# Two split stores, new list-scheduler priorities and two moved products in a fused scan and mixture-of-adapters kernel

## The chip, the cores and the metric

The kernel runs on one core of one Trainium2 chip. The metric is device time in microseconds (us) of one execution, smaller is better. The kernel before was timed in three runs, and one more execution was profiled.

## What is computed

Two stages follow one another. The first is a linear recurrence over time on a batch of 8 sequences of 6400 steps with 128 channels. The second takes each of the 51200 rows of its result as a token, picks the 2 best of 8 adapters for it, and adds the weighted low-rank (rank 16) products to the token.

```python
for t in range(S):                      # a, b: (8, 6400, 128)
    h = a[:, t] * h + b[:, t]
    out[:, t] = h
x = out.reshape(B * S, D)               # (51200, 128)
logits = x @ w_gate                     # 8 adapters
topk = two best of the 8 logits
w = softmax over these two
delta = sum over the two of w * ((x @ A[e]) @ B[e])
return x + delta
```

## The kernel before

**Tiling.** The 51200 rows are cut into 100 units of 512 rows (`UT`). Channels lie on the partitions while the recurrence runs, so that one VectorE scan instruction handles 512 steps of all 128 channels; a sequence has 12.5 units, so four units hold a boundary and take two scans.

**One unit's work**, by the names that the planner uses:

- `lda`, `ldb`: loads of a and b into rings of 8 slots (`RING`), two units (512 KB) per transfer except for a few at the start and the end, issued from SyncE's queue.
- `AB`: sixteen TensorE transposes that turn a and b into channel-major PSUM tiles (`pA`, `pB`).
- `aev`: ScalarE copies a from PSUM to `a_st`. `scan`: VectorE writes `xT` in fp16, a ring of 16 units (`XR`).
- `L`: four small matmuls give logits in `pTL`; `lev` copies the logits of a whole gating group to `Lg`.
- `gating`: per group of up to four units, m1, p1, p2, p3, m2, p4 to p7 on VectorE and GpSimd find the two best logits and the argument of a sigmoid (`sig`, ScalarE), which gives the weights `g`. In the groups with `quick` (the first three and the last two, `QUICK`) an eight-way maximum (`mx`) takes the place of m1 to m2, and the elementwise steps may go to either engine.
- `Z`: four matmuls with all the adapters' A at once. `mul`: the product with the weights, on VectorE out of PSUM, or, for the units in `POOL_MULS`, on GpSimd; GpSimd cannot read PSUM, so ScalarE first copies `Z` to `z_sb` (`zev`).
- `T`: four transposes of the weighted product; `tev`: ScalarE copies them to `zwT`.
- `R` and `D`: the tokens themselves and the adapters' B are accumulated in `pO`; `oev` copies the sum to a slot of `outt` (24 slots, `NOUT`). For the last ten units VectorE may take this copy too.
- `st`: stores of two units (512 KB), single units at the two ends, issued from SyncE's queue.

**The order.** Nothing is written out by hand. Every operation is put into a `_Plan` with its engine, a cost, what it depends on, and a key: its unit plus the offset of its kind in `KEY`, and, from unit `N_LATE` on, also that in `LATE`. `schedule` is a list scheduler. It takes the engine on which something can start soonest, looks at all that could start there within the engine's `SLACK` (ns) of that time, and emits the one with the smallest key:

```python
limit = soonest[e0] + self.slack.get(e0, 0.0)
t, op, e, pick = min((f for f in found if f[2] == e0 and f[0] <= limit), key=lambda f: (f[1].key, f[0]))
```

Each engine then runs its list in that fixed order and waits on semaphores where a dependency is on another engine. The costs only decide the order. TensorE's instructions are emitted through a helper (`_Parts`), so all its matmuls have line 90 and all its transposes line 94 in the profile.

**Groups.** `cut(HEAD, 4, TAILS)` makes the gating groups: the sizes in `HEAD` first, then fours for what is left, then the sizes in `TAILS`:

```python
rest = NU - u - sum(sizes_tail)
while rest > 0:
    n = min(size, rest)
```

**Stores.** The store that begins with unit `u0` waits for the copies of its units and, as long as `u0 + HOLD` (22) is smaller than `FREE`, also for the scan of unit `u0 + HOLD`, so that loads come first. The copy of unit `v` waits until the store of unit `v - 24`, which used the same slot, has landed.

Of the kernel before, what the change touches and what calls it, by code (L numbers as in the profile page):

```python
# [10 lines left out]


KEY = {
    "AB": -125.2, "aev": 74.6, "scan": 73.9, "L": -8.3, "lev": -133.3, "gate": 36.0, "sig": 65.6, "Z": 82.1,
    "mul": -166.5, "zev": 37.9, "T": -103.7, "tev": -4.9, "R": 173.0, "D": 58.8, "oev": 185.5,
}
SLACK = {
    "pe": 0.0, "dve": 20.0, "act": 0.0, "pool": 300.0, "sp": 200.0,
}
HEAD = (1, 1, 2, 1, 1, 3)  # L20
TAILS = (4, 3)
QUICK = (3, 2)
POOL_MULS = (2, 3, 5, 7, 10, 12, 14, 17, 22, 26, 30, 34, 38, 42, 46, 50, 54, 58, 62, 66, 70, 74, 78, 84, 89, 90)
HOLD = 22
FREE = 100
HEATS = 7
WIDE = 100
SOLO = (2, 4)
# [4 lines left out]
NOUT = 24  # L33
TAIL = 10
FILLS = 1
OUT4 = 86
LATE = {
    "L": -48.5, "zev": 113.4, "tev": -1.9, "aev": 21.0, "lev": -59.3, "sig": 6.0, "gate": 31.5, "AB": 19.8,
    "scan": -3.5, "mul": -20.9, "T": -31.3,
}  # L40
N_LATE = 80


class _Op:
# [55 lines left out]
class _Plan:  # L100
# [9 lines left out]
    def add(self, name, eng, kind, unit, cost, emit, deps=(), dma=None, bank=None, mode=None):  # L110

        engs = (eng,) if isinstance(eng, str) else eng
        cost = cost if isinstance(cost, dict) else {e: cost for e in engs}
        self.ops[name] = _Op(name, engs, kind, unit, cost, emit, list(deps), dma, bank, mode)

    def schedule(self, first, link, landing, switch):
# [3 lines left out]
        for op in ops.values():  # L120
            op.deps = [ops[d] for d in dict.fromkeys(op.deps) if d in ops]
            left[op.name] = len(op.deps)
            op.key = op.unit + self.offset.get(op.kind, 0.0)
            if op.unit >= N_LATE:
                op.key += LATE.get(op.kind, 0.0)
# [89 lines left out]
def bass_associative_scan_2x2__then__mixture_of_adapters_kernel(  # L215
# [8 lines left out]
    NB, S, D = a.shape  # L224
    E = moe_w_gate.shape[1]
    R = moe_A.shape[2]
# [8 lines left out]
    NZ, NO = 2, 2  # L235
    ON_POOL = lambda v: v in POOL_MULS

    def cut(sizes_head, size, sizes_tail):
        got, u = [], 0
        for n in sizes_head:  # L240
            got.append((u, n))
            u += n
# [3 lines that stand above are left out]
            got.append((u, n))  # L246
            u += n
            rest -= n
        for n in sizes_tail:
            got.append((u, n))  # L250
            u += n
        return got

    groups = cut(HEAD, 4, TAILS)
    GM = max(n for _, n in groups)
# [3 lines left out]
    with ExitStack() as stack:  # L259
# [20 lines left out]
        outt = sb(nc.sbuf_tensor("outt", [128, NOUT, UT], F32))  # L280
# [30 lines left out]
        def add_dma(name, eng, unit, starts, slot, time, deps=()):  # L311

            if slot not in dma_sem:
                dma_sem[slot] = [sb(nc.semaphore("q_" + "_".join(map(str, slot)))), 0]
            dma_sem[slot][1] += 16 * len(starts)
            sem, value = dma_sem[slot]

            def emit(h):
                for dst, src in starts:
                    last = h.dma_start(dst, src).then_inc(sem, 16)  # L320
                return last

            add(name, eng, "dma", unit, (450.0 * len(starts), 0.0), emit, deps, (sem, value, time))
# [54 lines left out]
        def fill(w):  # L378


            def emit(h):
                for _ in range(3):
                    last = h.matmul(pO[1][:, :], warm_t[:, 0:128], warm_t[:, :])
                return last

            add(f"fill{w}", "pe", "fix", 1000.0, (600.0, 800.0), emit, [f"AB{w}"])

        for w in range(FILLS):
            fill(w)
# [398 lines left out]
        def t_evac(v):  # L788
# [8 lines left out]
                bank=t_bank(v),  # L797
            )

        def o_bank(v):  # L800
            return pO[v % NO] if v < OUT4 else (pO + pB)[(v - OUT4) % 4]

        def o_free(v):
            if v < OUT4 + 2:
                return f"oev{v - NO}"
            return f"scan{NU - 2 + v % 2}" if v < OUT4 + 4 else f"oev{v - 4}"

        def delta(v):
            def emit(what):
                def run(h):  # L810
                    for q, w in [(q, w) for q in range(Q) for w in what]:
                        left, right = {"x": (x_rows(v, q), ident_h[:, :]), "d": (zw_rows(v, q), Bcat_h)}[w]
                        last = h.matmul(
                            o_bank(v)[:, q * 128 : (q + 1) * 128],
                            left,
                            right,
                            start=w == "x" and q == 0,
                            stop=w == "d",
                            skip_group_check=True,
                        )  # L820
                    return last

                return run

            deps = [f"scan{mates(v)[-1]}", o_free(v), "idh"]
            if v == 1:
                deps += [f"fill{w}" for w in range(5)]
            tevs = [f"tev{w}" for w in mates(v)]
            if FUSE[0] <= v < FUSE[1]:
                add(f"D{v}", "pe", "D", v, (WIDE8, WIDE8 + 200.0), emit("xd"), deps + tevs + ["cstB"], mode="full")  # L830
            else:
                add(f"R{v}", "pe", "R", v, (223.0, 423.0), emit("x"), deps, mode="full")
                add(f"D{v}", "pe", "D", v, (220.0, 420.0), emit("d"), [f"R{v}", "cstB"] + tevs, mode="full")

        def o_evac(v):
            def emit(h):
                copy = h.tensor_copy if plan.ops[f"oev{v}"].eng == "dve" else h.copy
                return copy(outt[:, v % NOUT, :], o_bank(v)[:, :])  # L838

            tail = v >= NU - TAIL  # L840
            add(
                f"oev{v}",
                ("act", "dve") if tail else "act",
                "oev",
                v,
                {"act": (477.0, 645.0), "dve": (600.0, 745.0)} if tail else (477.0, 645.0),
                emit,
                [f"D{v}", f"st{store_of.get(v - NOUT)}"],
            )

        stores, u = [], 0
# [3 lines left out]
        store_of = {v: j for j, (u0, n) in enumerate(stores) for v in range(u0, u0 + n)}  # L855

        def store(j):
            u0, n = stores[j]
            s0 = u0 % NOUT
            rows = out[u0 * UT : (u0 + n) * UT, :].rearrange("(p i) d -> p (i d)", p=128)  # L860
            add_dma(
                f"st{j}",
                "sp",
                u0 + HOLD,
                [(rows, outt[:, s0 : s0 + n, :].rearrange("p n c -> p (n c)"))],
                ("o", s0, n),
                1.036 * ((625.0 if n == 2 else 650.0) * n + 13.0),
                [f"oev{v}" for v in range(u0, u0 + n)] + [f"scan{u0 + HOLD}"] * (u0 + HOLD < FREE),
            )

        for w in range(NU):
            for t in "ab":
# [6 lines left out]
        for v in range(NU):  # L879
            logits(v)  # L880
            z_mm(v)
            z_mul(v)
            zw_tr(v)
            t_evac(v)
            delta(v)
            o_evac(v)
        for k in range(len(groups)):
            gating(k)
        for j in range(len(stores)):
            store(j)  # L890
        ends = [f"st{j}" for j in range(len(stores) - NOUT, len(stores))]
        add("end", "sp", "fix", 1.0e9, (10.0, 10.0), lambda h: h.nop(), ends)

        plan.schedule(700.0, 3000.0, lambda t: 400.0, 94.0)
# [49 lines left out]
```

## Time and profile before

| what | value |
|---|---|
| runs | 204.3, 205.97, 205.74 us; median 205.74 us |
| profiled execution, its own time | 204.61 us |
| its span | 202.5 us |
| busy share: PE, PEld, DVE, ACT, POOL | 94, 84, 92, 86, 56% |
| mean DMA rate | 392 GB/s, 79.35 MB |
| granted TensorE clock | 1.0 |

PE is TensorE's matmuls and transposes, PEld its weight loads, DVE is VectorE, ACT ScalarE, POOL GpSimd, SP SyncE. Times inside the profile count from the span's start. The span is what lies between the first and the last instruction; the execution's own time is 2.1 us longer. The DMA share is the mean over the core's 16 DMA engines. The busy time of TensorE is modelled, since its instructions overlap.

### The profile page before, as it was taken

What the parts mean: (1) busy time and instruction counts of PE and PEld (TensorE: products, weight loads), DVE (VectorE), ACT (ScalarE), POOL (GpSimd) and SP (SyncE); (2) the same over time, 40 slices, a digit from 0 to 9 for tenths busy, and PEclk for the clock granted to TensorE, in tenths of its full rate; (3) what the DMA queues carried; (4) which work ended last, traced back from release to release, by engine and by line L of the source; (5) the groups of instructions that cost most, each with busy time, mean ns of one, the idle gap of its engine ahead of it and who ended that gap; (6) DMA issues with size and microseconds to landing.
All of it is one profiled execution on the core that took longest, in us unless ns stands there. A gap on an engine that the chain in (4) does not pass through costs nothing.

```text
span 202.5 us, 8757 instructions
## 1 busy us (share of the span) xinstructions
PE 190.6 (94%) x3594; PEld 171.0 (84%) x3594; DVE 185.4 (92%) x286; ACT 174.8 (86%) x381; POOL 112.9 (56%) x220
## 2 busy tenths in 40 slices
PE   7878989899999999999999999999999999999890
PEld 3667878798899999999999999999999998998880
DVE  1599999989999999999999999999999999999990
ACT  3367867888999999999999999999999998989991
POOL 1326577858666656746756665574775664556200
PEclk9999999999999999999999999999999999999999
DMA  7999999999999999999999999999999999998695
GB/s 173 400 411 410 401 408 406 407 401 411 405 413 415 413 412 410 413 411 409 413 415 413 408 415 411 409 416 418 407 413 412 413 413 413 396 377 336 252 372 219
DMA packets 23687, 79.35 MB, mean 392 GB/s; under 512 B 3680, under 2 KB 3808, under 8 KB 23648
## 3 DMA queue, kind: packets, MB, share of 16 engines
q1 hardware_dynamic: 22320, 78.65, 97.3%
q8 instruction: 29, 0.48, 0.9%
q10 hardware_dynamic: 1328, 0.14, 0.5%
q14 instruction: 10, 0.08, 0.1%
HBM read 52.56 MB, written 26.21 MB: 389 GB/s over the span
## 4 chain that ended last, share of the span: by engine, by line
PE 79%; DVE 8%; ACT 5%; issue 2%; DMA 2%; SPq 0%; POOL 0%
PE pA L94 27%; PE pO L90 20%; PE pTL L94 13%; PE pZ L90 10%; PE pTL L90 5%; DVE xT L519 5%; PE pB L94 3%; ACT a_st L500 3%; DMA a_in<-in_a_dram 2%; PE pB L90 1%; ACT zwT L795 1%; DVE mx L598 1%; ACT outt L838 1%; DVE d L617 1%; DVE zw L738 0%
## 5 line engine op out<-in xcount | busy, mean ns | idle before, releaser
L519 DVE TENSOR_TENSOR_SCAN xT<-a_st,xT,pB 128x512 f16<-128x512 f32 x96 | 120.1, 1251 | 4.1 <-ACT a_st L500 1.1
L500 ACT COPY a_st<-pA 128x512 f32<-128x512 f32 x100 | 60.8, 608 | 19.4 <-PE pB L94 15.2
L94 PE MATMUL pA<-ident_f,a_in 64*128 64x64 f32 (+1 forms) x792 | 71.7, 230 | 3.4 <-ACT a_st L500 1.5
L94 PE MATMUL pB<-ident_f,b_in 64*128 64x64 f32 (+1 forms) x792 | 72.0, 230 | 0.4
L94 PEld LDWEIGHTS pA<-ident_f,a_in 64*128 64x128 f32 (+1 forms) x792 | 57.7, 139 | 12.1 <-ACT a_st L500 2.7
L795 ACT COPY zwT<-pTL 128x512 f16<-128x512 f16 x95 | 58.4, 615 | 0.1
L94 PEld LDWEIGHTS pB<-ident_f,b_in 64*128 64x128 f32 (+1 forms) x792 | 57.5, 138 | 0.9 <-issue 0.5
L838 ACT COPY outt<-pO 128x512 f32<-128x512 f32 x91 | 56.6, 627 | 1.1 <-PE pO L90 0.9
L738 DVE TENSOR_TENSOR zw<-pZ,g 128x512 f16<-128x512 f32 x74 | 50.0, 680 | 1.2 <-PE pTL L94 0.5
L90 PE MATMUL pO<-ident_h,xT 128*128 128x128 f16 x376 | 39.3, 227 | 0.1
L90 PE MATMUL pZ<-cst_h,xT 128*128 128x128 f16 x400 | 38.3, 219 | 0.0
L738 POOL TENSOR_TENSOR zw<-z_sb,g 128x512 f16<-128x512 f32 x26 | 27.5, 1062 | 18.9 <-PE pTL L90 15.5
L94 PE MATMUL pTL<-ident_h,zw 128*128 128x128 f16 x380 | 37.6, 221 | 0.0
L90 PE MATMUL pO<-cst_h,zwT 128*128 128x128 f16 x376 | 35.0, 217 | 0.9 <-ACT zwT L795 0.8
L90 PEld LDWEIGHTS pO<-ident_h,xT 128*128 128x128 f16 x376 | 31.1, 148 | 0.5 <-ACT outt L838 0.2
L90 PE MATMUL pTL<-cst_h,xT 128*128 128x8 f16 x400 | 27.5, 174 | 1.1 <-DVE xT L519 1.1
L90 PEld LDWEIGHTS pZ<-cst_h,xT 128*128 128x128 f16 x400 | 27.8, 114 | 0.2
L94 PEld LDWEIGHTS pTL<-ident_h,zw 128*128 128x128 f16 x380 | 21.9, 97 | 5.8
L90 PEld LDWEIGHTS pTL<-cst_h,xT 128*128 128x128 f16 x400 | 23.5, 117 | 2.4 <-DVE xT L519 1.6
L90 PEld LDWEIGHTS pO<-cst_h,zwT 128*128 128x128 f16 x376 | 22.5, 97 | 1.5 <-PE pO L90 1.0
L634 POOL TENSOR_TENSOR d<-Lg,m 128x128 f32<-128x128 f32 (+2 forms) x24 | 9.4, 392 | 22.4 <-DVE m L627 22.4
L669 POOL TENSOR_SCALAR pn<-d 128x128 f32<-128x128 f32 (+2 forms) x26 | 15.4, 593 | 2.3
(47 smaller groups left out, 148.9 us busy)
## 6 DMA issues: line engine op xcount, KB each, us to landing
a_in<-in_a_dram SPq DMA_DIRECT2D x49, 512.0 KB, 15.1
b_in<-in_b_dram SPq DMA_DIRECT2D x49, 512.0 KB, 15.0
out_dram<-outt SPq DMA_DIRECT2D x47, 512.0 KB, 14.6
out_dram<-outt SPq DMA_DIRECT2D x6, 256.0 KB, 3.6
a_in<-in_a_dram SPq DMA_DIRECT2D x2, 256.0 KB, 9.1
b_in<-in_b_dram SPq DMA_DIRECT2D x2, 256.0 KB, 4.4
cst_f<-in_moe_A_dram ACTq DMA_DIRECT2D x1, 64.0 KB, 4.1
cst_f<-in_moe_B_dram ACTq DMA_DIRECT2D x1, 64.0 KB, 5.2
```

The costliest lines, as they stand in the source:

```text
L90: return self.h.matmul(*args, **kw)
L94: return self.h.transpose(*args)
L500: lambda h: h.copy(a_st[w % 2][:, :], pA[0][:, :]),
L519: last = h.tensor_tensor_scan(out=x_at(lo, hi), data0=a_st[w % 2][:, lo:hi], data1=pB[w % 2][:, lo:hi], initial=init, op0=ALU.mult, op1=AL ...
L598: last = h.max(mx[s][:, j, :], Lg[s][:, j, :])
L617: lambda h: h.tensor_tensor(out=v(d1[s]), in0=v(Lg[s]), in1=first.to_broadcast([128, c, E]), op=ALU.subtract),
L634: lambda h: h.tensor_tensor(out=v(d1[s]), in0=v(Lg[s]), in1=bc(m1[s]), op=ALU.subtract),
L669: lambda h: h.tensor_scalar(v(pn[s]), v(d2[s]), 0.0, -1.0e30, ALU.is_lt, ALU.mult),
L738: lambda h: h.tensor_tensor(out=oview, in0=zview, in1=gview, op=ALU.mult),
L795: lambda h: h.copy(*evacuated(v)),
L838: return copy(outt[:, v % NOUT, :], o_bank(v)[:, :])
```

## The change

It changes five things.

1. The offsets of all kinds in `KEY` and in `LATE` have other values, `LATE` holds from unit 94 on instead of 80, and the slack of VectorE, GpSimd and SyncE is smaller.
2. `TAILS` is (3,) in place of (4, 3).
3. The products of units 9 and 19 move from VectorE to GpSimd, and those of units 12 and 17 from GpSimd to VectorE.
4. `FREE` is 92 in place of 100, so stores of units 70 to 76 no longer wait for a scan.
5. The stores that begin with units 66 and 72 are issued as two transfers each, of the first 68 and the last 60 of the 128 partitions, with a semaphore of their own; whoever waited for the store waits for both pieces (`pieces`).

```diff
 KEY = {
-    "AB": -125.2, "aev": 74.6, "scan": 73.9, "L": -8.3, "lev": -133.3, "gate": 36.0, "sig": 65.6, "Z": 82.1,
-    "mul": -166.5, "zev": 37.9, "T": -103.7, "tev": -4.9, "R": 173.0, "D": 58.8, "oev": 185.5,
+    "AB": -103.5, "aev": 151.5, "scan": 107.4, "L": -24.3, "lev": -267.4, "gate": 6.6, "sig": 46.9, "Z": 72.5,
+    "mul": -39.1, "zev": 110.1, "T": -303.2, "tev": -236.6, "R": 222.5, "D": 2.8, "oev": 335.8,
 }
 SLACK = {
-    "pe": 0.0, "dve": 20.0, "act": 0.0, "pool": 300.0, "sp": 200.0,
+    "pe": 0.0, "dve": 0.0, "act": 0.0, "pool": 200.0, "sp": 120.0,
 }
 HEAD = (1, 1, 2, 1, 1, 3)
-TAILS = (4, 3)
+TAILS = (3,)
...
-POOL_MULS = (2, 3, 5, 7, 10, 12, 14, 17, 22, 26, 30, 34, 38, 42, 46, 50, 54, 58, 62, 66, 70, 74, 78, 84, 89, 90)
+POOL_MULS = (2, 3, 5, 7, 9, 10, 14, 19, 22, 26, 30, 34, 38, 42, 46, 50, 54, 58, 62, 66, 70, 74, 78, 84, 89, 90)
 HOLD = 22
-FREE = 100
+FREE = 92
...
+SPLIT = {66: (68, 60), 72: (68, 60)}
 OUT4 = 86
 LATE = {
-    "L": -48.5, "zev": 113.4, "tev": -1.9, "aev": 21.0, "lev": -59.3, "sig": 6.0, "gate": 31.5, "AB": 19.8,
-    "scan": -3.5, "mul": -20.9, "T": -31.3,
+    "sig": -205.0, "L": 9.0, "AB": -68.5, "zev": 29.9, "oev": -39.1, "tev": -12.4, "mul": -15.8, "aev": 52.7,
+    "scan": 11.3, "T": 36.4, "R": 11.1,
 }
-N_LATE = 80
+N_LATE = 94
...
+        def pieces(j):
+            return [f"st{j}"] + [f"st{j}p{k}" for k in range(1, 8)]
...
-                [f"D{v}", f"st{store_of.get(v - NOUT)}"],
+                [f"D{v}"] + pieces(store_of.get(v - NOUT)),
...
+            slots = outt[:, s0 : s0 + n, :].rearrange("p n c -> p (n c)")
+            sizes = SPLIT.get(u0, (128,))
+            for k, size in enumerate(sizes):
+                part = slice(sum(sizes[:k]), sum(sizes[: k + 1]))
+                add_dma(
+                    f"st{j}p{k}" if k else f"st{j}",
+                    "sp",
+                    u0 + HOLD,
+                    [(rows[part], slots[part])],
+                    ("o", s0, n, k) if k else ("o", s0, n),
+                    1.036 * ((625.0 if n == 2 else 650.0) * n + 13.0) * size / 128,
+                    [f"oev{v}" for v in range(u0, u0 + n)] + [f"scan{u0 + HOLD}"] * (u0 + HOLD < FREE),
+                )
```

More of the change, by code (lines that the diff above doesn't have):

```diff
@@ L860, in store @@
             rows = out[u0 * UT : (u0 + n) * UT, :].rearrange("(p i) d -> p (i d)", p=128)
[L861 to L869, printed above, removed]
+            slots = outt[:, s0 : s0 + n, :].rearrange("p n c -> p (n c)")
[11 more added lines that the diff above has]
+                )
         for w in range(NU):
@@ L890, in bass_associative_scan_2x2__then__mixture_of_adapters_kernel @@
             store(j)
-        ends = [f"st{j}" for j in range(len(stores) - NOUT, len(stores))]
+        ends = [x for j in range(len(stores) - NOUT, len(stores)) for x in pieces(j)]
         add("end", "sp", "fix", 1.0e9, (10.0, 10.0), lambda h: h.nop(), ends)
```

## The prediction

> **What bounds the kernel now.** I read the page first: engine shares, the 40 slices, the DMA queues and the chain that ended last.
>
> ```profile
> span 202.5 us, 8757 instructions
> PE 190.6 (94%) x3594; PEld 171.0 (84%) x3594; DVE 185.4 (92%) x286; ACT 174.8 (86%) x381; POOL 112.9 (56%) x220
> DMA  7999999999999999999999999999999999998695
> q1 hardware_dynamic: 22320, 78.65, 97.3%
> PE 79%; DVE 8%; ACT 5%; issue 2%; DMA 2%; SPq 0%; POOL 0%
> ```
>
> Two things look full: TensorE (79% of the chain) and the DMA engines (97.3%). To see which one sets the end, and where TensorE still idles, I took windows by stage; columns are length, then busy time of PE, PEld, DVE, ACT, POOL, then clock, DMA share and GB/s.
>
> ```profile
> 6.00:54.00 48.00, 43.27 (x803) 36.94 (x802) 43.60 (x71) 36.31 (x84) 29.51 (x65) 1.00 1.03 406
> 54.00:176.00 122.00, 121.90 (x2433) 112.67 (x2430) 119.58 (x155) 116.00 (x253) 74.68 (x134) 1.00 1.03 412
> 184.00:188.00 4.00, 3.46 (x55) 3.04 (x53) 4.00 (x7) 3.66 (x8) 2.59 (x3) 1.00 0.86 343
> 191.00:192.00 1.00, 1.00 (x21) 1.00 (x19) 1.00 (x4) 1.00 (x4) 0.47 (x2) 1.00 0.09 33
> 176.00:200.40 24.40, 20.85 (x354) 19.24 (x350) 21.41 (x58) 20.38 (x43) 7.54 (x14) 1.00 0.86 341
> 200.40:201.20 0.80, 0.00 (x0) 0.00 (x0) 0.00 (x0) 0.00 (x0) 0.00 (x0) 1.00 0.06 23
> ```
>
> From 54 to 176 us TensorE idles 0.10 us of 122: the middle is TensorE's. Idle stands in the head (48.00 - 43.27 = 4.73 us) and in 184 to 188 (0.54). A full DMA share reads 1.03 here. After the arithmetic one more thing lasts: 0.06 of 16 engines is one engine, at work alone from 200.4 to 201.2. In 191 to 192 it was already so (0.09 of 16 is 1.4 engines). The stores say the same: each pair of rows is one store, its issue time and its landing after issue.
>
> ```profile
> L320 SPq DMA_DIRECT2D out_dram<-outt x1: 333/333/333, 165.0 to 165.0; - x1
> DMA to landing us min/median/max: 14.8/14.8/14.8
> L320 SPq DMA_DIRECT2D out_dram<-outt x1: 332/332/332, 176.0 to 176.0; - x1
> DMA to landing us min/median/max: 9.4/9.4/9.4
> L320 SPq DMA_DIRECT2D out_dram<-outt x1: 332/332/332, 188.0 to 188.0; - x1
> DMA to landing us min/median/max: 5.6/5.6/5.6
> L320 SPq DMA_DIRECT2D out_dram<-outt x1: 332/332/332, 198.5 to 198.5; - x1
> DMA to landing us min/median/max: 3.2/3.2/3.2
> ```
>
> The store of 188.0 lands at 193.6, across a stretch in which fifteen engines had almost nothing to do: one DMA engine runs late, and a store has landed only when its last engine has. The end is thus a near tie:
>
> ```profile
> 186.58 1.27 DVE L519 TENSOR_TENSOR_SCAN xT<-a_st,xT,pB 128x512 f16<-128x512 f32 x1
> 187.91 0.30 PE L90 MATMUL pTL<-cst_h,xT 128*128 128x8 f16 x4 [0.55 <-DVE xT L519]
> 197.45 0.38 PE L90 MATMUL pO<-cst_h,zwT 128*128 128x128 f16 x4 [0.39 <-ACT zwT L795]
> 197.87 0.59 ACT L838 COPY outt<-pO 128x512 f32<-128x512 f32 x1 [0.56 <-PE pO L90]
> ```
>
> The last copy ends at 198.46, its store issues at 198.5 and lands at 201.7; without the late engine it would land 0.8 us sooner, with the fifteen others.
>
> **The change, part by part.** The sum is made against the profiled execution's own time, 204.61 us (span 202.5 and 2.1 around it); that lies 1.1 us under the median of the runs shown, 205.74.
>
> *Group sizes: 0.* The words speak of last groups of 3, 3 and 2; the code does not make them. The head takes 9 units; before, 84 = 21 x 4 and then 4 and 3; after, 88 = 22 x 4 and then 3. Both give the same 29 groups, ending 4 and 3, and the same quick ones.
>
> *Priorities and slack: 0, bounds -2.8 and +1.9.* A key is unit plus offset. Sorted by engine the classes stay as they were, but for three swaps: TensorE's T now goes ahead of AB everywhere, ScalarE's sigmoid ahead of the product's copy (zev), and from unit 80 on zev ahead of a's copy (aev). The old tables hold both orders of each, one below unit 80 and one from there on, and the pace did not care:
>
> ```profile
> 121.25 0.40 PE L94 MATMUL pTL<-ident_h,zw 128*128 128x128 f16 x4
> 123.05 0.40 PE L94 MATMUL pTL<-ident_h,zw 128*128 128x128 f16 x4
> 177.33 0.40 PE L94 MATMUL pTL<-ident_h,zw 128*128 128x128 f16 x4
> 179.13 0.40 PE L94 MATMUL pTL<-ident_h,zw 128*128 128x128 f16 x4
> ```
>
> One unit takes 1.80 us under either order, so the middle costs nothing; its cover is that TensorE has no gap there, and a gap would cost its own length. Head and tail are open. There an order can win back at most TensorE's idle time, 4.73 us in the head and 0.55 + 0.39 before the end; it fills only what latencies leave, so 40% of the head's, 1.9, and all of the tail's 0.94 is my bound downwards, and the head's 1.9 lost instead the bound upwards. Nothing in these rows leans to either side, so I take 0.
>
> *Products 9 and 19 to GpSimd, 12 and 17 to VectorE: 0, bounds +-1.06.*
>
> ```profile
> L738 DVE TENSOR_TENSOR zw<-pZ,g 128x512 f16<-128x512 f32 x74 | 50.0, 680 | 1.2 <-PE pTL L94 0.5 <-PE pZ L90 0.5
> L738 POOL TENSOR_TENSOR zw<-z_sb,g 128x512 f16<-128x512 f32 x26 | 27.5, 1062 | 18.9 <-PE pTL L90 15.5
> L724 ACT COPY z_sb<-pZ 128x512 f32<-128x512 f32 x26 | 16.3, 625 | 0.0
> 184.04 2.13 POOL L738 TENSOR_TENSOR zw<-z_sb,g 128x512 f16<-128x512 f32 x2 [1.09 <-ACT g L693]
> ```
>
> GpSimd has 26 products before and after, so no engine's total moves. But 9 and 10 now stand in a row: 2.13 us as in the last line, and T of unit 10 waits up to 1.06 us more, while 12 comes sooner by about as much. The cover is the head's other TensorE work.
>
> *FREE 92: 0.* Stores of units 70 to 76 no longer wait for the scan 22 units later. Store 70 could go when unit 71 is copied; it went at 172.7.
>
> ```profile
> L838 ACT COPY outt<-pO x72: 587/612/687, 15.0 to 158.4; 128x512 f32<-128x512 f32 x72
> L320 SPq DMA_DIRECT2D a_in<-in_a_dram x1: 1073/1073/1073, 160.2 to 160.2; - x1
> DMA to landing us min/median/max: 15.3/15.3/15.3
> 182.00 0.61 PE L94 MATMUL pA<-ident_f,a_in 128*128 128x128 f32 x4
> ```
>
> The 72nd copy starts at 158.4, so that store may pass the last load on SP's queue. That load lands at 175.5, one store later 176.8, and is read at 182.0: 5 us of cover. Order does nothing for the late engine, which has no pause to fill; only fewer bytes help it.
>
> *Split stores: -0.8, bounds -0.8 and +4.3.* One 4 KB row costs an engine 0.973 x 16 x 202.5 us / 78.65 MB x 4096 B = 0.164 us; a whole store is 8 rows on each engine, 1.31 us. Two more issues cost SP 0.33 us each, in idle time. No transfer of 68 or 60 rows stands in the trace. If rows are spread evenly, 68 + 60 cost what 128 did: 0. If they are dealt in equal whole shares, 68 = 4 x 17 goes to four engines and 60 = 15 x 4 to fifteen. Then four engines carry 21 rows instead of 8 (+2.13 us a store, +4.3 for both), eleven carry 4 (-1.3 for both) and one none (-2.6). The late engine is one of sixteen, and twelve of these are relieved, by more than the 0.8 us that it costs; the gain stops at 0.8, where the last copy sets the end. I take that as nearest to the rows. Later copies into the two stores' slots have room: the store of 165.0 (unit 66) lands at 179.8, that of 176.0 (unit 72) at 185.4, the copies of units 90 and 96 come after 190.
>
> The Trainium skill (DMA: Bandwidth & Descriptors, "Why a DMA increments its semaphore by 16 and not by 1") states the equal shares: the largest number of engines up to 16 that divides the rows, from the lowest engine up. No run here shows it; by it the sum is -0.8 or the +4.3 of the rival below. The same page ("Latency and other measured facts") says that engines 7 and 15 are usually the slower ones. The trace agrees that one lags and does not name it; if it is 15, it carries no row of either split store.
>
> Sum: 204.61 - 0.8 = 203.8 us, 0.9% under the median.
>
> **Rivals.** *B, the split moves nothing that matters* (spread evenly, or another engine equally late): 204.6. For it: the store of 165.0 took 14.8 us, so a backlog is general. Against: only one engine works in 191 to 192.
>
> *C, slower: the engines with the 68 rows become the late ones.* Each gets +4.3 us. Between 176.0 and 200.4 the mean engine is idle 24.4 x (1 - 0.86/1.03) = 4.0 us, which absorbs it; it decides from an engine with less than 4.3 - 0.8 = 3.5 us idle among the four. With 1 us idle the end moves by 2.5 us (207.1); if the late engine is one of the four, by 4.3 (208.9). I price it at 208. For it: a mean of 4.0 is close to 3.5.
>
> *D, the new order also fills the head or the tail:* 203.8 less 1.9 is 201.9. For it: 4.73 us of idle there. Against: no row says that T or AB order caused it.
>
> *E, the order or the two GpSimd products in a row cost the head 1.9 to 3 us:* 206.5 to 207.9.
>
> **How the numbers follow.** Forecast A 0.36, B 0.12, C 0.22, D 0.18, E 0.12. One per cent of the median, about what a measurement of this kernel tells from no change, is 2.06 us: faster is under 203.7, slower over 207.8. A lies at that edge and is halved (0.18 and 0.18); D is faster; B is the same; C is slower in 0.16 and the same in 0.06; E 0.06 each. Faster 0.36, same 0.42, slower 0.22. The range takes in D with a little of its tail, and C and E but for their upper ends: 201.6 to 207.7. A's own, with +-1.06 for the products, is 202.7 to 204.9.
>
> **What would show it.** A: one or no engine alone after the last full DMA stretch, the last store landing about 2.4 us after issue instead of 3.2, span near 201.7, the pace still 1.80. C: a last stretch with a share of 0.2 to 0.25 (four engines) and a last landing over 5 us after issue. B: the one engine alone, as now. D or E: TensorE's busy time in 6 to 54 us away from 43.27. The forecast is wrong if the last copy ends more than 1 us from 198.5, or if the landing grows.

## The result, and the profile after

The changed kernel takes 203.77 us (median of 12 runs, 203.32 to 204.53), the kernel before 204.52 us (12 runs, 204.21 to 206.24). The ratio is 0.9957, with a 95% interval of 0.9937 to 0.9977: 0.75 us less, surely faster, and well inside one per cent. The forecast was 203.8. The profiled execution took 203.76 us for a span of 201.8.

The page of the changed kernel, in the order in which the page before was read:

```profile
span 201.8 us, 8755 instructions
PE 190.8 (95%) x3594; PEld 171.3 (85%) x3594; DVE 185.1 (92%) x286; ACT 174.4 (86%) x381; POOL 112.9 (56%) x220
DMA  6999999999999999999999999999999999998696
q1 hardware_dynamic: 22326, 78.65, 97.5%
PE 83%; DVE 8%; ACT 3%; issue 3%; POOL 1%; DVEq 0%
```

The engines' instruction counts are those of before and their busy times are within 0.4 us: no work went away. The queue of the loads and stores has the same bytes and six packets more. In the chain of work that ended last, DMA's 2% is gone and TensorE has 83% instead of 79%.

Windows by stage of the changed kernel (length, busy time of PE, PEld, DVE, ACT, POOL, clock, DMA share, GB/s):

```profile
6.00:54.00 48.00, 43.81 (x814) 37.41 (x813) 44.23 (x72) 35.74 (x84) 29.14 (x65) 1.00 1.03 407
54.00:176.00 122.00, 121.90 (x2429) 112.74 (x2427) 119.32 (x155) 116.60 (x254) 75.01 (x133) 1.00 1.03 412
200.00:200.40 0.40, 0.00 (x0) 0.00 (x0) 0.00 (x0) 0.00 (x0) 0.00 (x0) 0.78 0.07 26
200.40:200.80 0.40, 0.00 (x0) 0.00 (x0) 0.00 (x0) 0.00 (x0) 0.00 (x0) 0.50 0.01 5
```

The middle is the same to the hundredth (121.90 us of 122). The head gained 0.54 us of TensorE work (43.27 to 43.81). At the end one engine (0.07 of 16) still works alone, but from 200.0 and hardly beyond 200.4, where before it ran from 200.4 to 201.2.

The last copy and the last store of the changed kernel, from the timeline of ScalarE and from the rows of the store's line:

```profile
197.42 0.58 ACT L842 COPY outt<-pO 128x512 f32<-128x512 f32 x1 [0.56 <-PE pO L91]
```

```profile
L321 SPq DMA_DIRECT2D out_dram<-outt x1: 333/333/333, 198.0 to 198.0; - x1
DMA to landing us min/median/max: 2.8/2.8/2.8
```

The copy ends at 198.00 instead of 198.46, and its store lands 2.8 us after issue instead of 3.2. That is 0.8 us in all, but the two parts are not two gains: the late engine's end is one time, that of the last copy with its store another, and the later of them decides. The trace keeps them apart: each whole store leaves sixteen completion marks, one for each DMA engine. Of the last store before, fifteen are there by 200.83 and the sixteenth comes at 201.66. In the changed kernel fifteen are there by 200.40 and the sixteenth comes at 200.85. So the end moved by 0.81 us, and a single late engine still sets it.

It is not the same engine. The 68 rows of unit 72 leave four marks behind them, at 178.56, 179.75, 181.32 and 182.67, one for each engine that took part. The latest marks of the transfers that were issued next are these:

| transfer, by its issue | last mark | the mark before it |
|---|---|---|
| 68 rows of unit 72, 167.48 | 182.67 | 181.32 |
| 60 rows of unit 72, 167.82 | 183.29 | 181.95 |
| 168.47 | 184.54 | 183.21 |
| 168.94 | 185.82 | 184.44 |
| 169.70 | 187.04 | 185.71 |
| 173.68 | 188.29 | 186.94 |

An engine that works through its transfers in the order of their issue can have no mark earlier than the one it had before, and in each of these rows only the last mark comes late enough to belong to the engine of the row above. From there on other marks follow too, but at most 0.74 us after the one of the row above (0.2 us for the half-size stores at the very end), which is too soon: 8 rows take an engine 1.2 us and more here, and 0.6 in the half-size stores. So the same engine is the last one to the end, 200.85, at 1.25 us for each such store. The last engine of the changed kernel is thus one of the four that took the 68 rows, and the late engine of before now lands with the others.

### The profile page after: what moved, and what is told of

The parts are those of the page before. It is cut to its first block, busy times and chain, and to the rows that moved or that the text cites. A ratio compares the mean times of both kernels' runs of the same rounds, so it can differ in the third digit from the quotient of the medians.

```text
span 201.8 us, 8755 instructions
## 1 busy us (share of the span) xinstructions
PE 190.8 (95%) x3594; PEld 171.3 (85%) x3594; DVE 185.1 (92%) x286; ACT 174.4 (86%) x381; POOL 112.9 (56%) x220
## 4 chain that ended last, share of the span: by engine, by line
PE 83%; DVE 8%; ACT 3%; issue 3%; POOL 1%; DVEq 0%
PE pA L95 27%; PE pO L91 21%; PE pTL L95 13%; PE pZ L91 10%; PE pTL L91 5%; DVE xT L520 5%; PE pB L95 3%; PE pB L91 3%; ACT a_st L501 2%; DVE mx L599 1%; ACT zwT L796 1%; DVE d L618 1%; ACT outt L842 1%; DVE zw L739 1%; ACT g L694 0%
```

## The experiments

The chip runs gave these numbers; "last copy" is the end of the last copy to `outt`, "lands" the last completion mark of the last store, "behind" how much later it comes than the fifteenth, and "last engine" whose mark it is, followed through the marks as above: "old" is the late engine of before, "a loaded one" an engine that took a share of 68 rows. All this is from one profiled execution each. In the shared runs the kernel before had medians of 204.38 (e1 to e4), 204.47 (e5 to e8) and 204.39 us (e9 to e12).

| kernel | median us | ratio to before, 95% interval | last copy | lands | behind | last engine |
|---|---|---|---|---|---|---|
| before | 204.52 | | 198.46 | 201.66 | 0.83 | old |
| after | 203.77 | 0.9957, 0.9937 to 0.9977 | 198.00 | 200.85 | 0.45 | a loaded one |
| e1 split alone | 204.48 | 0.9996, 0.9975 to 1.0016 | 199.07 | 201.81 | 0.36 | a loaded one |
| e2 products alone | 204.34 | 0.9997, 0.9977 to 1.0017 | 198.29 | 201.68 | 1.00 | old |
| e3 FREE alone | 204.42 | 1.0007, 0.9991 to 1.0024 | 198.72 | 201.55 | 0.46 | old |
| e4 all but the split | 204.28 | 1.0001, 0.9985 to 1.0018 | 197.87 | 201.49 | 1.24 | old |
| e5 products and split | 204.68 | 0.9991, 0.9968 to 1.0015 | 197.82 | 202.01 | 1.06 | a loaded one |
| e6 split 120 + 8 | 204.77 | 1.0021, 1.0001 to 1.0041 | 198.17 | 201.81 | 1.26 | old |
| e7 split 64 + 64 | 204.69 | 1.0016, 0.9994 to 1.0038 | 198.34 | 201.69 | 0.87 | old |
| e8 thirteen stores 120 + 8 | 207.50 | 1.0164, 1.0122 to 1.0205 | 197.86 | 204.68 | 0.01 | not followed |
| e9 all but the priorities | 203.68 | 0.9971, 0.9950 to 0.9991 | 197.90 | 200.44 | 0.04 | one of these two |
| e10 all but FREE | 204.45 | 0.9994, 0.9969 to 1.0020 | 198.50 | 201.70 | 0.66 | a loaded one |
| e11 all, but units 9 and 12 as before | 203.88 | 0.9989, 0.9960 to 1.0017 | 199.63 | 202.02 | 0.03 | none is late |
| e12 split 100 + 28 | 205.97 | 1.0099, 1.0077 to 1.0121 | 198.12 | 202.97 | 0.31 | old and another |

The last copy of single executions wanders: the first scans of a profiled execution start up to 0.9 us apart. The landing does not wander with it: without a split it is 201.5 to 201.7 in four kernels (before, e2, e3, e4) whose last copies lie 0.85 us apart. That is what one engine looks like that has been busy all along and takes no notice of the arithmetic.

**e1, the split alone.** The kernel before with

```diff
+SPLIT = {66: (68, 60), 72: (68, 60)}
```

> The kernel before, with stores 66 and 72 as 68 and 60 rows and nothing else changed. Theory S (one DMA engine runs late to the end, and the split takes rows from it): the last copy still ends near 198.5 us in the span, the last store lands 2.8 us after its issue instead of 3.2, the span falls by 0.4 us to about 202.1, the ratio to before is about 0.998. Rival P (the whole gain is the moved products' work): nothing moves, 202.5 and 1.000. Rival C (the four engines with 68 rows become late): landing over 5 us, ratio over 1.01.

No gain: 0.9996. The last store of this kernel:

```profile
L321 SPq DMA_DIRECT2D out_dram<-outt x1: 332/332/332, 199.1 to 199.1; - x1
DMA to landing us min/median/max: 2.7/2.7/2.7
```

The landing is 0.5 us quicker after issue than before, which looks like the forecast. But the copy was 0.6 us later here, and the end, 201.8, is that of before. The marks say that the split did relieve the old late engine: fifteen are there by 201.45, as soon after the last issue as before. The sixteenth is an engine that took 68 rows: its mark of these rows of unit 72, at 186.12, is 2.5 us behind the other three, and it is the last one from there to the end.

**e2, the products alone.** The kernel before with

```diff
-POOL_MULS = (2, 3, 5, 7, 10, 12, 14, 17, 22, ...
+POOL_MULS = (2, 3, 5, 7, 9, 10, 14, 19, 22, ...
```

> The kernel before, with the products of units 9 and 19 on GpSimd and those of 12 and 17 on VectorE, and nothing else changed. Theory: the last copy ends 0.4 to 0.5 us sooner, near 198.0, but the late DMA engine still has all its rows, so the last store lands about 3.6 us after its issue and the span stays at 202.5 (ratio 1.000). Rival P (the products alone give the gain): the landing stays at 3.2 and the span falls to 202.0, ratio 0.998.

No gain: 0.9997. The last copy is a little sooner, and the store takes that much longer:

```profile
L321 SPq DMA_DIRECT2D out_dram<-outt x1: 333/333/333, 198.3 to 198.3; - x1
DMA to landing us min/median/max: 3.4/3.4/3.4
```

198.3 + 3.4 is 201.7 again.

**e3, FREE alone.** The kernel before with

```diff
-FREE = 100
+FREE = 92
```

> The kernel before with FREE 92 alone: stores 70 to 76 no longer wait for scans. Theory: the late DMA engine has no pause to fill, so nothing moves: span 202.5, ratio 1.000, last landing 3.2 us. Rival F (the late engine does pause in the last 25 us, and earlier stores fill the pause): landing 2.8 and span 202.1, ratio 0.998.

No gain: 1.0007.

**e4, everything but the split.** The changed kernel with

```diff
-SPLIT = {66: (68, 60), 72: (68, 60)}
+SPLIT = {}
```

> The kernel after without the two splits (every store in one piece); new keys, products and FREE stay. Theory: last copy near 198.0 as after, but the last landing is 3.6 us after issue instead of 2.8, so the span is 202.5 against 201.8 after and the ratio to before 1.000. Rival P: as after, 201.8 and 0.996.

The whole gain is gone: 1.0001, an interval that does not touch that of the changed kernel. Its last copy is even sooner than the changed kernel's (197.87), and its last store waits for the old late engine:

```profile
L321 SPq DMA_DIRECT2D out_dram<-outt x1: 332/332/332, 197.9 to 197.9; - x1
DMA to landing us min/median/max: 3.6/3.6/3.6
```

So the split is needed (e4) and does not do it alone (e1). What it needs beside it was the next question.

**e5, products and split.** The kernel before with `SPLIT` of e1 and `POOL_MULS` of e2, and `FREE` still 100.

> The kernel before with two edits only, the four moved products and the two splits into 68 and 60 rows; old keys, slack, LATE, TAILS and FREE 100. Theory M (two things end together, the arithmetic and one late DMA engine, and each edit moves one of them): together they give the whole gain, ratio to before 0.996, about 203.6 us, last landing 2.7 to 2.8 us after issue. Rival (FREE 92 is needed beside them, since the stores must start sooner): ratio 1.000.

No gain that can be told: 0.9991. The rows of the stores, of the second 68 rows and of the last three:

```profile
L321 SPq DMA_DIRECT2D out_dram<-outt x1: 279/279/279, 175.3 to 175.3; - x1
...
L321 SPq DMA_DIRECT2D out_dram<-outt x3: 737/983/1087, 196.4 to 198.5; - x3
DMA to landing us min/median/max: 3.5/4.0/4.3
```

An issue that took 0.33 us before takes 0.7 to 1.1 us in these three, so the last store leaves at 198.5 although its copy ended at 197.82. It lands at 202.0. The second store in two pieces lands at 186.9; the store in its place landed at 185.4 before. The last engine is again one of the four with 68 rows (marks of unit 72 at 181.08, 182.37, 183.90 and 186.33), and this kernel differs from e9 below only by `FREE`.

**e10, everything but FREE.** The changed kernel with

```diff
-FREE = 92
+FREE = 100
```

> The kernel after with FREE 100: only stores 70 to 76 wait for scans again, so the 68 rows of unit 72 go out near 175 us and not near 167. Theory F2 (the four engines with 68 rows need the earlier start, since they can then work their extra rows off in the pause after 176 us): as in the run with the minimal edits, ratio 0.998 to 1.000, single executions from 203.3 up to 206, last landing above 3 us or its issue delayed. Rival M (FREE is not needed, and that run was disturbed): ratio 0.996 and executions between 203.3 and 204.5, as after.

0.9994: the gain is gone here too. Its last store, and the window after the last load:

```profile
L321 SPq DMA_DIRECT2D out_dram<-outt x1: 799/799/799, 198.6 to 198.6; - x1
DMA to landing us min/median/max: 3.2/3.2/3.2
```

```profile
176.00:180.00 4.00, 4.00 (x84) 3.73 (x82) 3.92 (x6) 3.70 (x8) 1.51 (x3) 1.00 0.90 352
```

The same window of the changed kernel, and its second issue of 68 rows:

```profile
176.00:180.00 4.00, 4.00 (x82) 3.67 (x81) 4.00 (x7) 3.70 (x8) 1.51 (x3) 1.00 1.01 391
```

```profile
L321 SPq DMA_DIRECT2D out_dram<-outt x1: 298/298/298, 167.5 to 167.5; - x1
```

With `FREE` 100 the second 68 rows go out only at 175 to 177 us (175.3 in e5, 176.0 in e10, 176.6 in e1), when engines already run dry: the share from 176 to 180 is 0.90, against 1.01. With `FREE` 92 both pairs of pieces are out by 167.8, and the share stays full until 180. One of the four is the last engine here and in the changed kernel alike. What differs is how long that engine took for its 17 rows of unit 72, counted from its mark before: at least 3.8 us in e10, 4.0 in e1 and 4.2 in e5, but at most 3.2 in the changed kernel and 2.8 in e9, where 17 rows at 0.164 us are 2.8. So with `FREE` 100 this engine takes longer over the piece, by about 0.6 us or more. Why it does isn't shown: in e10 the piece had been issued about 6 us before the engine reached it, so it did not wait for the issue. The two comparisons that differ by `FREE` alone (after with e10, e9 with e5) both favour 92, by 0.0037 and 0.0020; the intervals of each pair overlap, so it is the two pairs and the landings (200.85 and 200.44 against 201.70 and 202.01) that carry this. Single executions scatter more with `FREE` 100, too: 203.27 to 206.84 us in e5 and 203.39 to 205.37 in e10, against 203.32 to 204.53 in the changed kernel, although one execution of e9 also took 205.75.

**e9, everything but the priorities.** The changed kernel with the old `KEY`, `SLACK`, `TAILS`, `LATE` and `N_LATE`.

> The kernel after with the old KEY, SLACK, TAILS, LATE and N_LATE; the moved products, FREE 92 and the two splits stay. Theory K (the new priorities change next to nothing in the engines' lists): as after, ratio to before 0.996, last landing 2.8 us after its issue. Rival (the priorities carry part of the gain): ratio 0.998 to 1.000.

0.9971, not to be told from the changed kernel's 0.9957. The new priorities bring nothing that these runs can see. The instruction lists say why: against e2's kernel, the changed one has the same order on TensorE, VectorE and GpSimd, and on ScalarE two swaps of neighbours. The last store of this execution lands soon after its issue, with the sixteenth mark only 0.15 us behind the fourteenth:

```profile
L321 SPq DMA_DIRECT2D out_dram<-outt x1: 332/332/332, 197.9 to 197.9; - x1
DMA to landing us min/median/max: 2.5/2.5/2.5
```

**e6 and e7, other cuts of the same two stores.** The changed kernel with

```diff
-SPLIT = {66: (68, 60), 72: (68, 60)}
+SPLIT = {66: (120, 8), 72: (120, 8)}    # e6
+SPLIT = {66: (64, 64), 72: (64, 64)}    # e7
```

> The kernel after with stores 66 and 72 as 120 and 8 rows in place of 68 and 60. If whole shares are dealt to the lowest engines, fifteen engines carry 8 rows as ever, eight of them one more, and only the last one carries none. Theory L (the late engine is that last one): it is relieved of 16 rows as by 68 and 60, last landing 2.7 to 2.8 us after issue, ratio 0.996. Rival (the late engine is one of those that 68 and 60 relieved by half): no relief, landing 3.6, span 202.4, ratio 1.000.

> The kernel after with stores 66 and 72 as 64 and 64 rows: two pieces each, but 4 rows on every engine from each piece. Theory (the dealing of rows matters, not the number of pieces): no relief, last landing 3.5 to 3.8 us after issue, span 202.4, ratio 1.000. Rival (smaller pieces alone help): 0.996.

Neither gains (1.0021 and 1.0016), and both land as the kernel before does, 201.81 and 201.69. The last store of e6, and the queue's rows of the pages of e6 and of e7 (packets, MB, share):

```profile
L321 SPq DMA_DIRECT2D out_dram<-outt x1: 332/332/332, 198.2 to 198.2; - x1
DMA to landing us min/median/max: 3.6/3.6/3.6
```

```profile
q1 hardware_dynamic: 22334, 78.65, 97.0%
```

```profile
q1 hardware_dynamic: 22352, 78.65, 97.2%
```

These counts and the marks show how rows are dealt. The bytes and the rows are the same in every kernel, so a different count can only come from the one small packet by which each engine taking part reports that it is done. A whole store has 16 of them; two split stores have 2 x (p + q - 16) more, with p and q engines in the pieces. The changed kernel has 6 more than the 22320 of before, which is 4 + 15; e6 has 14 more, which is 15 + 8; e7 has 32 more, which is 16 + 16. The marks agree one by one: a piece of 68 rows leaves four marks behind the one at its issue, a piece of 60 fifteen, a piece of 8 eight. So equal whole shares it is: 68 rows go to four engines with 17 each, 60 to fifteen with 4. The Trainium skill says the same in "DMA: Bandwidth & Descriptors", "Why a DMA increments its semaphore by 16 and not by 1", and the counts agree with it. That the lowest-numbered engines are the ones used is the Trainium skill's alone: no count names an engine.

With e7 every engine gets what it got before, and the end stays. With e6 one engine is spared all 8 rows twice, and the end stays too: the spared one is not the late one. The marks say more. The 120 rows of unit 66 have their last mark at 181.14, 0.9 us behind the mark before it, and the 8 rows that follow have one at 181.34: the late engine is one of the eight that got a row more. Its two extra rows are 0.33 us, and the end is 0.32 us behind that of e4, which has no split.

**e12, ten engines loaded.** The changed kernel with

```diff
-SPLIT = {66: (68, 60), 72: (68, 60)}
+SPLIT = {66: (100, 28), 72: (100, 28)}
```

> The kernel after with stores 66 and 72 as 100 and 28 rows. By equal whole shares 100 goes to ten engines (10 rows each) and 28 to fourteen (2 rows each): ten engines carry 12 rows, 4 more than in one piece (0.66 us a store), the next four 2, the last two none. If the late engine is one of the upper six and the ten lower ones have 1.3 us to spare, last landing 2.4 to 2.6 us after issue and ratio 0.994 to 0.996, the better version. If the late engine is among the ten, it gets 1.3 us later: landing over 4.5 us and ratio 1.005.

One per cent slower. Its page and its last three stores:

```profile
q1 hardware_dynamic: 22336, 78.65, 96.7%
```

```profile
L321 SPq DMA_DIRECT2D out_dram<-outt x3: 1064/1084/1091, 196.7 to 198.9; - x3
DMA to landing us min/median/max: 4.1/4.6/5.0
```

16 packets more are 2 x (10 + 14 - 16): ten engines with 10 rows, fourteen with 2. Ten engines thus have 12 rows instead of 8, which at 0.164 us a row is 1.31 us for two stores, and the last store lands 1.31 us later than before (202.97 against 201.66). Two engines are late here, not one: fourteen marks are there by 201.66, the last two come at 202.66 and 202.97. The last two marks of the 100 rows of unit 72 are at 183.83 and 184.51, and both engines stay behind the others from there on. The one with 183.83 needs 1.37 us for each of the next six stores (184.17 to 192.40), the pace of the late engine before, which took 1.38 (181.23 to 193.66, nine stores); the other needs 1.25, the pace of the loaded engine in the changed kernel. So the old late engine is one of the ten. It is not one of the four: in the changed kernel the store ahead of the first 68 rows has its last mark at 179.80, and the four marks of the 68 rows behind it are all there by 178.34.

By the rule of the lowest engines in the Trainium skill ("DMA: Bandwidth & Descriptors", "Why a DMA increments its semaphore by 16 and not by 1") it would be one of numbers 4 to 7, since e6 has it among the eight. The same page of the Trainium skill ("Latency and other measured facts") names 7 and 15 as usually slower; 7 would fit, and e6 and e12 speak against 15.

**e8, many stores.** The changed kernel with `(120, 8)` for the thirteen stores of units 66, 68, ... to 90.

> The kernel after with all stores from unit 66 to unit 90 as 120 and 8 rows. Under theory L the last engine is relieved of 13 stores' rows and is never late; the end is set by the arithmetic and the fastest landing, 2.4 us after issue, so 0.4 us less than after, ratio to before 0.994, with a risk that the eight engines with one row more per store (13 rows, 2.1 us) end later. If L is wrong: landing over 3.5 us and ratio 1.000 or more.

1.6% slower. The last five stores:

```profile
L321 SPq DMA_DIRECT2D out_dram<-outt x5: 639/901/1070, 197.3 to 201.2; - x5
DMA to landing us min/median/max: 3.5/4.3/4.7
```

The last copy ended at 197.86, the last store was issued at 201.2. Thirteen times one row more on eight engines (13 x 0.164 = 2.1 us each) makes them late, SyncE is held for up to 1.07 us at an issue, and the stores pile up behind it: the last one lands 3.0 us later than before, 0.9 us more than the rows alone.

**e11, units 9 and 12 as before.** The changed kernel with

```diff
-POOL_MULS = (2, 3, 5, 7, 9, 10, 14, 19, 22, ...
+POOL_MULS = (2, 3, 5, 7, 10, 12, 14, 19, 22, ...
```

> The kernel after with only the second pair of products moved: 19 to GpSimd and 17 to VectorE, while 9 stays on VectorE and 12 on GpSimd. Theory (the 0.5 us of the moved products comes near 45 to 52 us of the span, which is where unit 19 passes): the scans run 0.5 us ahead of before from 54 us on and the ratio is 0.996, as after. Rival (it is 9 in place of 12): no lead, ratio 0.998 to 1.000.

Its times do not decide: a median of 203.88, a ratio of 0.9989 with an interval that holds both the changed kernel's and no change. Its profile tells two things. The first is on the late engine. No engine is late at the end, which alone would say little, because the last copy is 1.2 us later here than before. But of the store issued at 189.21 fifteen marks are there by 191.99, and the sixteenth, at 193.64, is again of an engine with 68 rows, which has caught up one store later. The old late engine is thus relieved without the pair of 9 and 12, and in e1 without any of the moved products. The second is that the step which the products make in the head is absent. Scans on VectorE's timeline in the kernel before, in the changed kernel and in e11, the first of them at the same place of the program:

```profile
42.33 1.27 DVE L519 TENSOR_TENSOR_SCAN xT<-a_st,xT,pB 128x512 f16<-128x512 f32 x1
...
45.46 1.28 DVE L519 TENSOR_TENSOR_SCAN xT<-a_st,xT,pB 128x512 f16<-128x512 f32 x1 [0.48 <-PE pTL L90]
...
51.81 1.27 DVE L519 TENSOR_TENSOR_SCAN xT<-a_st,xT,pB 128x512 f16<-128x512 f32 x1
```

```profile
42.33 1.27 DVE L520 TENSOR_TENSOR_SCAN xT<-a_st,xT,pB 128x512 f16<-128x512 f32 x1
...
51.34 1.27 DVE L520 TENSOR_TENSOR_SCAN xT<-a_st,xT,pB 128x512 f16<-128x512 f32 x1
```

```profile
43.12 1.27 DVE L520 TENSOR_TENSOR_SCAN xT<-a_st,xT,pB 128x512 f16<-128x512 f32 x1
...
46.25 1.28 DVE L520 TENSOR_TENSOR_SCAN xT<-a_st,xT,pB 128x512 f16<-128x512 f32 x1 [0.48 <-PE pTL L91]
...
52.62 1.27 DVE L520 TENSOR_TENSOR_SCAN xT<-a_st,xT,pB 128x512 f16<-128x512 f32 x1
```

Between 42 and 52 us the changed kernel gains 0.47 us on the kernel before, and a scan's wait of 0.48 us on TensorE is gone; in e11 that wait is back and the distance of the scans is that of before (9.50 us against 9.48; 9.01 in the changed kernel). e2, e4, e5 and e9 have the step too, e1 and e3 do not. Whether the pair of 9 and 12 does it alone or only together with 19 and 17 wasn't tried.

## Why the prediction was right, and where it was not

The time (203.77 for 203.8) and the sum (-0.8) came out, and the late engine was relieved by the mechanism that the prediction names. That the size came out is in part luck: what stopped the gain is not what the prediction said. The four zeros hold for each edit by itself; the zero of `FREE` does not hold beside the split.

*Group sizes 0, priorities 0.* Right. e9 without them is as fast, and neither the filling of the head and tail (rival D) nor the damage (rival E) came from the order.

*Products 0, bounds +-1.06.* The size was off. The arithmetic ends about 0.5 us sooner: the head has 0.54 us more TensorE work in 6 to 54 us, the mark that the prediction gave for rival D, with a quarter of D's 1.9 us and from another edit. I had the head's idle time as cover on both sides and did not follow VectorE's wait at 45.46 us back to the product ahead of it. It costs the forecast nothing, because a late engine hides it: e2 alone is 0.9997, and in the changed kernel fifteen engines wait from 200.40 to 200.85 for the sixteenth.

*Split -0.8, "the gain stops at 0.8, where the last copy sets the end".* The relief is as named, and the equal whole shares are shown by the packet counts and the marks. But what stopped the gain was not the last copy, and it was not the old late engine either, which is spared 8 rows, 1.3 us by the prediction's own price, and lands with the others by 200.40. It was one of the four engines with 68 rows, at 200.85. The step that failed is "the mean engine is idle 24.4 x (1 - 0.86/1.03) = 4.0 us, which absorbs it": the mean did not hold for this engine, and 0.45 us of its extra rows stand at the end. The prediction had this as rival C, with a price of 3 us and more; it came, at a small size, together with the forecast. The predicted landing of 2.4 us after issue was 2.8 therefore, while the span came out (201.8 for 201.7), because the last copy was 0.46 us sooner than forecast: two misses of about the same size cancelled. In e9 the loaded engine is nearly in time, and the last mark comes at 200.44, 1.2 us sooner than before.

*FREE 92: 0.* This step failed too. "Order does nothing for the late engine, which has no pause to fill" is true, and e3 shows it. It is not true of the engines that take over the rows. The prediction priced rival C without asking when the 68 rows arrive; with `FREE` 100 those of unit 72 arrive at 175 to 177, and one of the four engines then ends as late as the old one did. With the split and without `FREE` 92 the gain is absent (e1 0.9996, e5 0.9991, e10 0.9994). The forecast took two terms as independent, and came out because the change makes both edits. Why the engine takes longer over rows that are issued later stays open.

*Rivals.* B, that the split moves nothing because another engine is equally late, is what e1, e5 and e10 do. C is real in the same way: one of the four is the last engine in those three and in the changed kernel. Loading more engines costs 1.0% and 1.6% (e12, e8). E's upper end was added wrongly: 204.61 + 3 is 207.6 and not 207.9.

The best of the tried kernels are the changed one and e9, which can't be told apart; no version was clearly better than both kernels. The split with `FREE` 92 and all products in the old places was not run, so whether the products are needed for the 0.4% stays open; e11 is the nearest, and its interval holds both answers.

## What to carry to other kernels

When a store lands in a stretch where the DMA share shows one engine of sixteen, look for the engine that is late, not for bytes in all: a faster order of the arithmetic brings nothing until that engine is relieved, and the landing time that stays put while the last copy moves is its mark. A transfer cut into unequal pieces shifts rows between engines, and the engines that take them over can be the next late ones: here one of them was the last in four of the six kernels with 68 + 60, and at a later time when the rows were issued later. So price the idle time of the engine that is loaded, not that of the mean one, and follow the completion marks to see which engine ends last; that the end is late by one engine does not say that it is the same one. Two edits that each measure zero alone can be the two halves of one gain, so test by leaving each one out of the whole too, and not only by adding each to the start.

## What the runs showed of the hardware that was not expected

One of the sixteen engines is slower than others at the same rows. In the kernel before, its marks from 181.23 to 193.66 come 1.38 us apart, for stores of 8 rows to an engine; the loaded engine of the changed kernel takes 1.25 us for the same (184.54 to 193.32). Every engine leaves its mark on a whole store, so by equal shares each has 8 rows of it: this one is late by its pace and not by its load.

The issue of a store in the tail takes 0.33 us before and in the changed kernel, and in some of the last stores up to 0.80 us in e10 and 1.07 to 1.09 us in e5, e8 and e12. The stores leave later by it: 0.7 us for the last one in e5 and over 3 us in e8. In these four kernels engines are behind; but e4 and e6 end with one engine 1.2 us behind and issue in 0.33 us, so what makes an issue long is not shown.

And 4 rows more in each of two stores move the end by as much as their bytes say: 1.31 us later with 100 + 28.
